# An earlier square root, read-outs moved to VectorE and a check's sums moved into the second pair: a Fourier-mixing and SwiGLU block on one core

## The chip, the cores and the metric

The kernel runs on one core of a Trainium2 chip. The metric is the device time of one execution in microseconds (us). A profile is one further execution, recorded by the hardware profiler. In its rows PE is TensorE (matmuls) and PEld its weight loads, DVE is VectorE, ACT is ScalarE, POOL is GpSimd and SP is SyncE, which here only issues transfers.

## The reference

One row block x of 2048 x 512 goes through two sublayers. All of it is float32.

```python
mod = (_silu(c) @ w_mod).reshape(c.shape[0], 6, 1, -1)
sa, ca, ga, sb, cb, gb = ...               # six vectors of 512
h = _layernorm(x) * (1 + ca) + sa
x = x + ga * (Cr @ h @ Wr - Ci @ h @ Wi)   # real part of a two-dimensional DFT
h = _layernorm(x) * (1 + cb) + sb
x = x + gb * ((silu(h @ w1) * (h @ w3)) @ w2)      # w1, w3: 512 x 1792, w2: 1792 x 512
```

The DFT matrices Cr, Ci (2048 x 2048) and Wr, Wi (512 x 512) are inputs. The kernel uses their mirror symmetry to halve the work, and a check computes whether the inputs have it; if not, a second program, `general`, runs behind the first.

## The kernel before, in words

Each float32 product is made of three matmul passes over a high and a low part: the high part is a rounded copy (ACT, `copy`, L87), the low part is the difference (DVE, `minus`, L90). In the rows `hf`, `h2h`, `th`, `w1h` and so on are such pairs: `h2h`/`h2l` are the two halves of the second layer norm's result, `th`/`tl` are sums of such blocks.

The sequence of 2048 is cut into four blocks t = 0 to 3 of 512 columns; each block is held transposed in two tiles (i = 0, 1) of 128 x 1024. The blocks form two pairs, (0, 2) and (1, 3). "The third block" is t = 2, the second member of the first pair. The hidden width 1792 is cut into seven groups g of 256.

After the DFT, `ln2(t)` computes the second layer norm of a block as a list of small steps: sums over rows and partitions, the square root of the variance (`a6`, ACT, L880, with a table load ahead of it), the reciprocal and its spread (`a6b`, DVE, L883 to L848, tile `stat`), the multiplication of the two tiles by it (`a7`, DVE, `xc`, L96), scale and shift (`a8`, ACT, `xc`, L894), and then the rounding into `h2h` and `h2l` (`chunk_parts`). These steps stand in a queue called `background`. Between the units of PE work the program calls `advance`, which takes steps from that queue as long as a credit in microseconds for DVE and ACT is left; a `pause` ends one call. This decides where a step lands among the other instructions of its engine. Every engine then works strictly in the order in which it was given its instructions. Tiles come from 50 slots that are reused first in, first out, so an instruction that moves also changes which slot a later tile gets.

PE's work around the change is, in this order:

- first products of the first pair, plainly: `up(0,0)`, `up(1,0)` (block 0, groups 0 and 1), eight second products `down` of block 0, then `up(0,2)`, `up(1,2)` (block 2). A second product is six matmuls into one of the PSUM banks 4 to 7, and its result is read out and scaled by `gb` into a tile `y` (ACT, `copy_by`, L335), which POOL's queue adds to DRAM (L1146).
- then twelve `items` (a group g for a pair of blocks). An item has seven products of w1 (a1 to a7) and seven of w3 (b1 to b7) instead of eight each, with sums of weights and of blocks made on DVE. Between them stand eight second products "y" of the item before, now in the two banks 6 and 7 alone. A unit is six matmuls. The order of one item is fixed by a string: `-b7 a1 a2 -b4 -b3 a6 a5 y a7 y y a4 y a3 y b1 y b2 y b6 b5 y`, where a minus marks the item before. a6 adds to the bank of a1, a7 to that of a6 and a4 to that of a7, so each of them starts when ACT or DVE has read what the bank held; b6, b7 and b4 likewise. Items 0 to 4 are the first pair, items 5 to 11 the second.

Of block 1 and block 3 the layer norm runs in the background of items 0 to 2 and 2 to 4.

`judge` (L1003 to L1026) adds up the squares that the check collected: one clearing of a tile by POOL and fifteen small DVE instructions, each of which waits for the one before, ending in the flag `bad`, which is read when everything else is done.

The lines that follow the steps in the profile:

```python
            (0, partition_sums, 1.0, 0.0),
            pause,
            (0, a6, 0.0, 2.8),
            pause,
            (0, a6b, 1.6, 0.0),
```

Of the kernel before, what the change touches and what calls it, by code (L numbers as in the profile page):

```python
# [12 lines left out]
OP = mybir.AluOpType  # L13
# [9 lines left out]
ND = D // P  # L23
# [19 lines left out]
def folded(nc, pools, c, cp, wmr, wmc, x, xt, ctr, cti, wdr, wdi, w1, w3, w2, out):  # L43
# [51 lines left out]
    def times(dst, a, b):  # L95
        nc.vector.tensor_tensor(out=dst, in0=a, in1=b, op=OP.mult)  # L96
# [13 lines left out]
    background = deque()  # L110
# [3 lines left out]
    def step(queue, slots, fn, dve=0.0, act=0.0):  # L114
        queue.append((slots, dve, act, fn))
# [176 lines left out]
    gb = consts.tile([P, ND], F32, name="gb")  # L292
# [41 lines left out]
    def copy_by(dst, src, by):  # L334
        nc.scalar.activation(dst, src, AF.Identity, scale=by)  # L335
# [477 lines left out]
    PAIRS = ((0, 2), (1, 3))  # L813
# [3 lines left out]
    def ln2(t):  # L817
# [69 lines left out]
        def a7(i):  # L887
            rstd = v["s"][:, 1, :].unsqueeze(1).to_broadcast([P, 2, N])
            times(xc[t, i], xc[t, i], rstd)

        def a8(i):
            for q in range(2):
                e = 2 * i + q
                nc.scalar.activation(  # L894
                    xc[t, i][:, q, :],
                    xc[t, i][:, q, :],
                    AF.Identity,
                    bias=sb[:, e : e + 1],
                    scale=cb1[:, e : e + 1],
                )  # L900
# [12 lines left out]


        apart = t != PAIRS[0][0]
        pause = (0, None, 0.0, 0.0)
        for slots, fn, dve, act in (
            (2, a1, 1.2, 0.0),
            (0, a1b, 0.7, 0.0),
            (0, rows, 1.3, 0.0),  # L920
            (1, partition_sums, 1.0, 0.0),
            (1, a2, 1.5, 0.0),
            (1, lambda: a3(0), 1.2, 0.0),
            *[pause] * apart,
            (1, lambda: a3b(0), 0.0, 1.0),
            (1, lambda: a3(1), 1.2, 0.0),
            *[pause] * apart,
            (1, lambda: a3b(1), 0.0, 1.0),
            (0, keep, 0.0, 0.0),
            pause,  # L930
            (0, a4, 1.2, 0.0),
            (0, a1b, 0.7, 0.0),
            (0, rows, 1.3, 0.0),
            (0, partition_sums, 1.0, 0.0),
            pause,
            (0, a6, 0.0, 2.8),
            pause,
            (0, a6b, 1.6, 0.0),
            (0, lambda: a7(0), 1.2, 0.0),
            *[pause] * apart,  # L940
            (0, lambda: a8(0), 0.0, 1.4),
            (0, lambda: a7(1), 1.2, 0.0),
            *[pause] * apart,
            (0, lambda: a8(1), 0.0, 1.4),
            (0, a9, 0.0, 0.0),
        ):
            step(background, slots, fn, dve * (1.4 if apart else 1.0), act)

    def chunk_parts(queue, t, i, more=0):
        def highs():  # L950
            h2h[t, i] = take(F32R, "h2h")
            copy(flat(h2h[t, i]), flat(xc[t, i]))

        def lows():
            h2l[t, i] = take(F32R, "h2l")
            minus(flat(h2l[t, i]), flat(xc[t, i]), flat(h2h[t, i]).bitcast(F32))
            done.add(("h2", t, i))

        step(queue, 1 + more, highs, 0.0, 1.0)
        step(queue, 1, lows, 1.2, 0.0)  # L960

# [150 lines left out]
    ys = {}  # L1112
    down_banks = [4, 4]

    def down_unit(g, pair, t, d, key):
        last = g == NG - 1

        own = pair == 1 and g >= NG - 2
        if not own and d % 2 == 0:
            ys[0] = take(F32, "y")  # L1120

        parts = 2 if own and last and (t, d) == (NT - 1, ND - 1) else 1
        for n in range(parts):
            at = slice(n * N // parts, (n + 1) * N // parts)
            to = bank(down_banks[0] + turn[1] % down_banks[1])[:, at]
            turn[1] += 1
            for q in range(2):
                product(
                    to,
                    [u[:, q, cols(d)] for u in wuse[key]],  # L1130
                    [hf[g, t, q][:, b, at] for b in range(2)],
                    q == 0,
                    q == 1,
                )
            if own:
                xs = xr[t][d // 2][:, d % 2, at]
                nc.vector.scalar_tensor_tensor(
                    xs, to, gb[:, d : d + 1], xs, op0=OP.mult, op1=OP.add
                )
                if last:  # L1140
                    nc.sync.dma_start(out[t, d, :, at], xs)
            else:
                copy_by(ys[0][:, d % 2, :], to, gb[:, d : d + 1])
        if not own and d % 2 == 1:
            y = ys.pop(0)
            nc.gpsimd.dma_start(sums[t, d // 2], y, accum_op=OP.add)  # L1146
            behind(4, lambda: give(y))
            if last:
                behind(8, lambda i=d // 2: store(t, i))
        if d == ND - 1:  # L1150
            for q in range(2):
                give(hf.pop((g, t, q)))
            if t == PAIRS[pair][1]:
                give_w(key)
            if pair == 1 and g == NG - 3:
                load_sums(t)
# [366 lines left out]
    for n, (j, k) in enumerate(steps):  # L1523
        if k == 2:
            load_xt(j + 2)
        if k == 5:
            load_xt(j)
        for m in range(2):
            if todo and todo[0] == (n, m):
                prepare_some(1, n)  # L1530
            if (k, m) == (NK // 2 - 1, 1):
                drain(lambda: ("mod", 0) in done)
            seq_unit(n, m, last_rows if (n, m) == (0, 0) else None)
            load_some(n + 3)
            prepare_some(2 if n == 0 else 1, n + 2)
            square_seq()
            load_some(n + 4)
            if (j, k, m) == (0, NK - 1, 1):
                for t in PAIRS[0]:
                    ln2(t)  # L1540
                    for i in range(2):
                        chunk_parts(background, t, i, 1)
                sum_parts(background, *pair_sums(background, 0))

            if k % (NK // 2) != NK // 2 - 1 or m == 1:
                advance(2.2 if todo else 5.0)
        if n == len(steps) - 3:
            load_w(("w1", 0))
            load_w(("w3", 0))
        if n == len(steps) - 2:  # L1550
            for w in ("w1", "w3"):
                w_high((w, 0))
                w_low((w, 0))
# [40 lines left out]
    for g in range(2):  # L1594
        for d in range(ND):
            down(g, 0, 0, d, ("w2", g))
    judge()
    up(0, 2)
    load_w(("w3", *items[0]))
    weight_jobs(0, "w1")  # L1600
# [8 lines left out]
    turning = len([at for at in items if at[1] == 0])  # L1609
# [11 lines left out]
    def unit(kind, i, n):  # L1621
        g, pair = items[i]
        more = i + 1 < len(items)
# [7 lines left out]
            drain(lambda: ("t", 1, {6: 2, 5: 1, 7: 3, 4: 4}[n]) in done, jobs)  # L1631
        delayed()
        factor(i, "w1" if kind == "a" else "w3", n)
        if (kind, n) == ("a", 1) and more:
            load_w(("w1", *items[i + 1]))
        if (kind, n) == ("a", 6):
# [843 lines left out]
```

## Time and profile before

| | |
|---|---|
| time, three runs | 710.34, 712.18 (median), 712.77 us |
| the profiled execution's own time | 708.46 us |
| its span, first to last instruction | 706.7 us |
| PE busy / weight loads | 686.3 us (97%) / 564.7 us (80%) |
| DVE busy | 548.3 us (78%) |
| ACT busy | 430.8 us (61%) |
| POOL busy | 119.4 us (17%) |
| mean granted TensorE clock | 0.991 |

A row of the timeline gives the start, the duration, the engine, the source line, the operation and the tiles ("out<-in"), and in square brackets how long the engine stood idle before it and what released it. A matmul of 512 columns is recorded with 0.39 us, but they are pipelined: a new one starts every 0.227 us, and the time PE loses is seen in the distance from start to start. The chain of waits follows the end of the program back from instruction to instruction. Stretches of time ("windows") give busy time, number of instructions and granted clock.

### The profile page before, as it was taken

The page shows a single profiled execution, that of the slowest core. Times are in us where ns is not written, and L with a number is a line of the kernel's source. Part 1 is how long each engine was busy: PE and PEld are TensorE (multiplying, and loading weights), DVE is VectorE, ACT ScalarE, POOL GpSimd, SP SyncE. Part 2 cuts the span into 40 slices and gives each one's busy share as a digit, 9 for nine tenths or more (in the row PEclk, how much of TensorE's full clock was granted, in tenths as well). Part 3 has the DMA queues.
Part 4 walks back from the last instruction along what each step waited for, and adds up shares of the span by engine and source line. Part 5 has one row for each costly group of instructions (what it writes and reads, how often), then busy time and mean ns, then how long its engine had stood idle before and what let it go on. Part 6 is the DMA issues. An engine that isn't in the chain of part 4 may idle for free.

```text
span 706.7 us, 8912 instructions
## 1 busy us (share of the span) xinstructions
PE 686.3 (97%) x3152; PEld 564.7 (80%) x3152; DVE 548.3 (78%) x877; ACT 430.8 (61%) x709; POOL 119.4 (17%) x141
## 2 busy tenths in 40 slices
PE   7999999999999999899999999999999999999995
PEld 4898888888888888687888788787788888888784
DVE  5999679997999978579987886896865556664763
ACT  4998865545454655745677676867665565656420
POOL 1320253542524000200100101011010100101000
PEclk9999999999999999999999999999999999999998
DMA  8730299796678521522868558376763847537403
GB/s 266 211 120 1 77 373 328 251 307 229 207 283 287 168 86 41 92 58 64 209 114 199 89 130 153 61 156 137 239 136 73 180 62 175 111 69 162 137 0 124
DMA packets 38100, 108.93 MB, mean 154 GB/s; under 512 B 4896, under 2 KB 5152, under 8 KB 38048
## 3 DMA queue, kind: packets, MB, share of 16 engines
q0 software_dynamic: 12352, 43.00, 29.3%
q1 hardware_dynamic: 25264, 63.98, 27.5%
q10 hardware_dynamic: 432, 1.31, 0.5%
q8 instruction: 26, 0.43, 0.3%
q14 instruction: 26, 0.21, 0.1%
HBM read 76.81 MB, written 33.55 MB: 156 GB/s over the span
## 4 chain that ended last, share of the span: by engine, by line
PE 81%; DVE 7%; ACT 6%; issue 2%; DMA 2%; SPq 1%; ACTq 0%; DVEq 0%
PE bank L100 52%; PE bank L750 25%; PE bank L559 2%; PE bank L598 1%; DMA wmr<-in_wmr 1%; ACT xc L894 1%; PE bank L576 1%; DVE xc L96 1%; SPq L231 1%; ACT hf L87 1%; ACT y L335 1%; DVE v L96 0%; DVE hl L90 0%; ACT hm L501 0%; DMA w<-in_wdi 0%
## 5 line engine op out<-in xcount | busy, mean ns | idle before, releaser
L100 PE MATMUL bank<-hf,w2h 128*128 128x512 f32 (+1 forms) x452 | 140.9, 391 | 0.3
L1146 POOL DMA_DIRECT2D sum<-y x48 | 41.0, 855 | 390.1 <-ACT y L335 373.0
L100 PEld LDWEIGHTS bank<-hf,w2h 128*128 128x128 f32 x452 | 84.3, 188 | 22.1 <-DVE hf L90 3.4
L100 PE MATMUL bank<-hf,w2l 128*128 128x512 f32 (+1 forms) x226 | 87.6, 388 | 0.0
L87 ACT ACTIVATE hf<-v 128x512 fp32r<-128x512 f32 x56 | 35.3, 630 | 67.3 <-DVE v L96 62.7
L335 ACT ACTIVATE y<-bank,gb 128x512 f32<-128x512 f32 x96 | 64.9, 682 | 18.6 <-PE bank L100 18.3
L93 DVE TENSOR_TENSOR v<-bank,x 128x512 f32<-128x512 f32 x36 | 24.7, 685 | 34.9 <-PE bank L100 34.8
L750 PE MATMUL bank<-bh,us 128*128 128x512 f32 x128 | 49.9, 390 | 0.0
L93 DVE TENSOR_TENSOR x<-bank,x 128x512 f32<-128x512 f32 x36 | 24.7, 687 | 32.4 <-PE bank L100 28.7
L750 PE MATMUL bank<-bh,ul 128*128 128x512 f32 x128 | 49.8, 389 | 0.0
L750 PE MATMUL bank<-d,us 128*128 128x512 f32 x128 | 49.8, 389 | 0.0
L750 PE MATMUL bank<-d,uh 128*128 128x512 f32 x128 | 49.8, 389 | 0.0
L750 PE MATMUL bank<-l,us 128*128 128x512 f32 x128 | 49.8, 389 | 0.0
L750 PE MATMUL bank<-l,uh 128*128 128x512 f32 x128 | 49.8, 389 | 0.0
L100 PEld LDWEIGHTS bank<-hf,w2l 128*128 128x128 f32 x226 | 42.4, 188 | 8.4
L90 DVE TENSOR_TENSOR hf<-v,hf 128x512 fp32r<-128x512 f32 x56 | 38.5, 687 | 12.2 <-ACT hf L87 12.1
L170 POOL DMA_INDIRECT re<-in_ctr,mirror x32 | 35.8, 1117 | 66.2 <-DVE ul L90 39.5
L1224 ACT ACTIVATE v<-v 128x512 f32<-128x512 f32 x36 | 22.8, 632 | 38.8 <-DVE v L93 38.8
L87 ACT ACTIVATE x<-bank 128x512 f32<-128x512 f32 x72 | 41.4, 586 | 7.2 <-PE bank L100 6.5
L170 POOL DMA_INDIRECT im<-in_cti,mirror x32 | 32.7, 1023 | 35.3 <-PE bank L750 10.0
L100 PE MATMUL bank<-h2h,w1h 128*128 128x512 f32 x80 | 31.8, 397 | 1.5 <-ACT h2h L87 1.5
L100 PE MATMUL bank<-h2l,w1h 128*128 128x512 f32 x80 | 31.9, 399 | 0.8 <-DVE h2l L90 0.8
(246 smaller groups left out, 1775.2 us busy)
## 6 DMA issues: line engine op xcount, KB each, us to landing
sum<-y POOLq DMA_DIRECT2D x48, 512.0 KB, 5.6
w<-in_w SPq DMA_DIRECT2D x42, 512.0 KB, 4.5
re<-in_ctr SPq DMA_DIRECT2D x32, 256.0 KB, 5.0
im<-in_cti SPq DMA_DIRECT2D x32, 256.0 KB, 5.0
wmc<-in_wmc SPq DMA_DIRECT2D x8, 512.0 KB, 6.3
xr<-in_xt SPq DMA_DIRECT2D x8, 512.0 KB, 7.6
sum<-xr SPq DMA_DIRECT2D x8, 512.0 KB, 6.2
x<-in_x SPq DMA_DIRECT2D x11, 256.0 KB, 4.8
```

Of the source, the lines that this page charges most:

```text
L87: nc.scalar.activation(dst, src, AF.Copy, scale=scale)
L90: nc.vector.tensor_tensor(out=dst, in0=a, in1=b, op=OP.subtract)
L93: nc.vector.tensor_tensor(out=dst, in0=a, in1=b, op=OP.add)
L96: nc.vector.tensor_tensor(out=dst, in0=a, in1=b, op=OP.mult)
L100: nc.tensor.matmul(acc, lhs[a], rhs[b], start=first and n == 0, stop=last and n == len(PASSES) - 1, skip_group_check=more,)
L170: nc.gpsimd.indirect_dma_start(dst, None, rows, bass.IndirectOffsetOnAxis(ap=at, axis=0))
L231: queue.dma_start(raw_w[dt][q * 64 : (q + 1) * 64, m, :], w[i][par::2, q])
L335: nc.scalar.activation(dst, src, AF.Identity, scale=by)
L559: nc.tensor.matmul(halves(hb[k])[:, m, :], sides((hh, hl)[a][k])[:, dt, m, :], wu[dt][:, b, m, :], start=False, stop=dt % 2 == 1 and n == ...
L750: nc.tensor.matmul(acc[what, e], lhs, rhs, start=begin and i == 0, stop=(end or (turn and what == "x")) and i == len(terms) - 1, skip_grou ...
L1146: nc.gpsimd.dma_start(sums[t, d // 2], y, accum_op=OP.add)
L1224: behind(k != 0 or q == 0, lambda: nc.scalar.activation(v, src, AF.Silu))
```

## The change

Only the order of some work and the engine of eight read-outs change; what is computed stays as it was.

1. In `ln2(2)` (`rushed`), the pause ahead of the square root is gone, a pause is put behind `a6b`, and the costs of `a7` and `a8` are set to zero. The rounding of the block comes as `chunk(t, i)`, high part and low part as separate steps between pauses: the first tile is rounded as soon as its scale and shift is done, instead of after both.
2. Of the eight second products of the first pair in groups 0 and 1, numbers 1 to 4 (counted from 0) of each block are read out by DVE (`tensor_scalar`, L1153) in place of ACT. This holds for block 0 (ahead of `up(0,2)`) and for block 2 (in item 0).
3. `judge()` is called behind unit b4 of item 6, which is run at the head of item 7, in place of ahead of `up(0,2)`.

```diff
         apart = t != PAIRS[0][0]
+        rushed = t == PAIRS[0][1]
         pause = (0, None, 0.0, 0.0)
...
             (0, partition_sums, 1.0, 0.0),
-            pause,
+            *[pause] * (not rushed),
             (0, a6, 0.0, 2.8),
             pause,
             (0, a6b, 1.6, 0.0),
-            (0, lambda: a7(0), 1.2, 0.0),
-            *[pause] * apart,
-            (0, lambda: a8(0), 0.0, 1.4),
-            (0, lambda: a7(1), 1.2, 0.0),
-            *[pause] * apart,
-            (0, lambda: a8(1), 0.0, 1.4),
+            *[pause] * rushed,
+            (0, lambda: a7(0), 1.2 * (not rushed), 0.0),
+            *[pause] * (apart and not rushed),
+            (0, lambda: a8(0), 0.0, 1.4 * (not rushed)),
+            (0, lambda: a7(1), 1.2 * (not rushed), 0.0),
+            *([(0, fn, 0.0, 0.0) for fn in (None, chunk(t, 0)[0], None)] if rushed else [pause] * apart),
+            (0, lambda: a8(1), 0.0, 1.4 * (not rushed)),
             (0, a9, 0.0, 0.0),
         ):
             step(background, slots, fn, dve * (1.4 if apart else 1.0), act)
-
-    def chunk_parts(queue, t, i, more=0):
+        if rushed:
+            for fn in (chunk(t, 0)[1], None, chunk(t, 1)[0], None, chunk(t, 1)[1], None):
+                step(background, 0, fn)
+
+    def chunk(t, i):
...
+        return highs, lows
+
+    def chunk_parts(queue, t, i, more=0):
+        highs, lows = chunk(t, i)
...
             else:
-                copy_by(ys[0][:, d % 2, :], to, gb[:, d : d + 1])
+                if pair == 0 and 1 <= g * ND + d <= 4:
+                    nc.vector.tensor_scalar(
+                        ys[0][:, d % 2, :], to, gb[:, d : d + 1], None, op0=OP.mult
+                    )
+                else:
+                    copy_by(ys[0][:, d % 2, :], to, gb[:, d : d + 1])
...
                     ln2(t)
-                    for i in range(2):
+                    for i in range(2 if t == PAIRS[0][0] else 0):
                         chunk_parts(background, t, i, 1)
...
             down(g, 0, 0, d, ("w2", g))
-    judge()
     up(0, 2)
...
         factor(i, "w1" if kind == "a" else "w3", n)
+        if (kind, i, n) == ("b", turning + 1, 4):
+            judge()
```

Three places of the order show what this moves. The first is ACT during the eight second products of block 0, from the table load of the third block's square root on (`s` is that root, `xc` the scale and shift, `y` a read-out). Before:

```order
L880 ACT_TABLE_LOAD
L880 ACTIVATE s_377_2721<-s_377_2721,eps 32x16
L335 ACTIVATE y_2743<-bank_382_2744,gb 128x512
L335 ACTIVATE y_2743<-bank_383_2759,gb 128x512
L335 ACTIVATE y_2769<-bank_385_2770,gb 128x512
L894 ACTIVATE xc_2564<-xc_2564,sb,cb_151 128x512 x2
L335 ACTIVATE y_2769<-bank_386_2780,gb 128x512
L335 ACTIVATE y_2790<-bank_388_2791,gb 128x512
L894 ACTIVATE xc_2611<-xc_2611,sb,cb_151 128x512 x2
L335 ACTIVATE y_2790<-bank_389_2801,gb 128x512
L335 ACTIVATE y_2810<-bank_391_2811,gb 128x512
L87 ACTIVATE h2h_2819<-xc_2564 128x1024
```

ACT at the same place in the changed program:

```order
L880 ACT_TABLE_LOAD
L880 ACTIVATE s_377_2721<-s_377_2721,eps 32x16
L87 ACTIVATE hf_2738<-v_2714 128x512
L335 ACTIVATE y_2750<-bank_382_2751,gb 128x512
L894 ACTIVATE xc_2564<-xc_2564,sb,cb_151 128x512 x2
L87 ACTIVATE h2h_2772<-xc_2564 128x1024
L894 ACTIVATE xc_2611<-xc_2611,sb,cb_151 128x512 x2
L87 ACTIVATE h2h_2796<-xc_2611 128x1024
```

The load and the root now stand ahead of the copy `hf`, which they followed before, and one read-out instead of six stands between the root and the first `h2h`.

The second place is DVE in item 0, around its sums for block 1's layer norm (`xr`, `t`, `r`) and the addition `v` that empties bank 0 of a7 for a4. Before:

```order
L90 TENSOR_TENSOR w3l_3045<-w_406_2925,w3h_3030 128x1024
L90 TENSOR_TENSOR tl_3049<-xc_2259,th_3012 128x1024
L90 TENSOR_TENSOR w3sl_3061<-w3s_3032,w3sh_3047 128x1024
L805 SCALAR_TENSOR_TENSOR xr_2313<-sum_2539,ga,xr_2313 128x512 x2
L805 SCALAR_TENSOR_TENSOR xr_2019<-sum_2539,ga,xr_2019 128x512 x2
L93 TENSOR_TENSOR v_3026<-bank_426_3017,x_3070 128x512
L805 SCALAR_TENSOR_TENSOR xr_2314<-sum_2540,ga,xr_2314 128x512 x2
L805 SCALAR_TENSOR_TENSOR xr_2020<-sum_2540,ga,xr_2020 128x512 x2
L93 TENSOR_TENSOR t_3115<-xr_2313,xr_2314 128x1024
L93 TENSOR_TENSOR t_3115<-t_3115 128x512
```

DVE there in the changed program:

```order
L90 TENSOR_TENSOR w3sl_3045<-w3s_3018,w3sh_3033 128x1024
L805 SCALAR_TENSOR_TENSOR xr_2314<-sum_2540,ga,xr_2314 128x512 x2
L805 SCALAR_TENSOR_TENSOR xr_2020<-sum_2540,ga,xr_2020 128x512 x2
L93 TENSOR_TENSOR v_3012<-bank_427_3003,x_3054 128x512
L93 TENSOR_TENSOR t_3076<-xr_2313,xr_2314 128x1024
L1153 TENSOR_SCALAR y_3058<-bank_444_3079,gb 128x512
L1153 TENSOR_SCALAR y_3088<-bank_446_3089,gb 128x512
L93 TENSOR_TENSOR t_3076<-t_3076 128x512
L826 STREAM_TRANSPOSE t_3076<-t_3076 128x512
L828 TENSOR_REDUCE r_446_3099<-t_3076 128x16
L1153 TENSOR_SCALAR y_3088<-bank_447_3108,gb 128x512
```

One `tl` and half of the `xr` rows have moved ahead of this place, and the read-outs `y` have come in.

The third place is DVE at the head of item 7, behind unit b4 of item 6 (`v<-v,bank` empties its bank; `x<-bank` and the next `v` belong to b3; `hf` is the low part of b4's result). Before:

```order
L96 TENSOR_TENSOR v_4584<-v_4584,bank_738_4731 128x512
L93 TENSOR_TENSOR x_4738<-bank_748_4783,x_4738 128x512
L96 TENSOR_TENSOR v_4583<-v_4583,x_4738 128x512
L93 TENSOR_TENSOR w3s_4853<-w_731_4708 128x256
L90 TENSOR_TENSOR w3s_4853<-w3s_4853,w_731_4708 128x256
L90 TENSOR_TENSOR w3s_4853<-w_731_4708 128x256
L90 TENSOR_TENSOR w3s_4853<-w_731_4708,w3s_4853 128x256
L90 TENSOR_TENSOR hf_4841<-v_4584,hf_4841 128x512
```

In the changed program the same rows stand behind the check's sums, whose last five rows are shown:

```order
L1030 TENSOR_SCALAR own<-sq 1x4
L1032 TENSOR_TENSOR fine<-sq,own 1x4
L96 TENSOR_TENSOR fine<-fine 1x2
L96 TENSOR_TENSOR fine<-fine 1x1
L1035 TENSOR_SCALAR bad<-fine 1x1
L93 TENSOR_TENSOR x_4718<-bank_748_4763,x_4718 128x512
L96 TENSOR_TENSOR v_4563<-v_4563,x_4718 128x512
L93 TENSOR_TENSOR w3s_4853<-w_731_4688 128x256
L90 TENSOR_TENSOR w3s_4853<-w3s_4853,w_731_4688 128x256
L90 TENSOR_TENSOR w3s_4853<-w_731_4688 128x256
L90 TENSOR_TENSOR w3s_4853<-w_731_4688,w3s_4853 128x256
L90 TENSOR_TENSOR hf_4841<-v_4564,hf_4841 128x512
```

All of the check's sums now stand between the `v` of b4 and the low part `hf` of b4's result.

## The prediction

> **What bounds the kernel now.** The first view is the page's line of busy times, the next the waits of PE and of its weight loads.
>
> ```profile
> PE 686.3 (97%) x3152; PEld 564.7 (80%) x3152; DVE 548.3 (78%) x877; ACT 430.8 (61%) x709; POOL 119.4 (17%) x141
> ```
>
> ```profile
> PE bank L100 <- ACT x L87: 1.2, 3, 0.5
> ...
> PEld bank L100 <- DVE hf L90: 3.4, 9, 0.5
> ```
>
> PE is busy for 97% of the span. An edit on DVE or ACT therefore counts only where PE waits for it, or would begin to. The two rows of waits, both short and repeated, say that PE waits where ACT has not yet emptied a bank, and where DVE has not yet made the low part `hf` that a second product needs. The largest single wait is the one the change is about, at the start of `up(0,2)`. The timeline of PE has it:
>
> ```profile
> 294.80 0.39 PE L100 MATMUL bank<-hf,w2l 128*128 128x512 f32 x1
> 296.71 0.51 PE L100 MATMUL bank<-h2h,w1h 128*128 128x512 f32 x1 [1.53 <-ACT h2h L87]
> 297.97 0.79 PE L100 MATMUL bank<-h2l,w1h 128*128 128x512 f32 x1 [0.76 <-DVE h2l L90]
> ...
> 301.03 0.39 PE L100 MATMUL bank<-h2h,w1l 128*128 128x512 f32 x1
> ```
>
> Without a wait the next matmul starts 0.227 us behind the last. From 294.80 to 296.71 PE loses 1.91 − 0.23 = 1.68 us, from 296.71 to 297.97 another 1.26 − 0.23 = 1.03. From 297.97 to 301.03 there are seven starts in 3.06 us where 7 × 0.227 = 1.59 would do: 1.47 lost with no wait shown. The windows tell why (stretch, length, PE busy and its count, those of PEld, DVE, ACT and POOL, granted clock, DMA share, GB/s):
>
> ```profile
> 7.37:10.78 3.41, 2.15 (x11) 1.26 (x10) 1.99 (x7) 2.57 (x6) 0.00 (x0) 1.00 1.04 395
> 10.78:14.19 3.41, 2.32 (x17) 1.95 (x17) 3.30 (x5) 1.85 (x4) 0.00 (x0) 1.00 1.06 257
> ...
> 294.09:297.50 3.41, 1.60 (x6) 0.75 (x4) 0.81 (x1) 3.41 (x6) 0.85 (x1) 1.00 1.00 157
> 297.50:300.91 3.41, 2.94 (x7) 2.36 (x8) 2.73 (x7) 1.96 (x2) 1.03 (x2) 0.50 1.10 177
> ```
>
> The granted clock changes in steps of 3.41 us. A step with 1.81 us of PE idle (53%) was followed by one at 0.50, a step with 1.26 idle (37%) by one at full clock. So a stall here has a second price of 1.47, once it fills about half of such a step. All told this place costs 1.68 + 1.03 + 1.47 = 4.2 us.
>
> **The earlier root and rounding.** The chain of waits that ends in that stall:
>
> ```profile
> 284.41 0.70 DVE v L96
> ...
> 285.78 1.28 ACT L880
> ...
> 287.08 0.32 ACT s L880
> ...
> 290.49 1.10 ACT xc L894 x2
> ...
> 291.92 1.24 ACT y L335 x2
> 293.16 1.41 ACT xc L894 x2
> ...
> 295.61 1.06 ACT h2h L87
> 296.69 1.24 DVE h2l L90
> ```
>
> The sums over which the root is taken are done when DVE turns to `v` at 284.41. The table load nevertheless waits behind `hf` until 285.78. In the changed order load and root stand ahead of `hf`, and the load (1.28) fits in ahead of 284.4, so that the root starts at about 284.4 instead of 287.08, 2.7 sooner. Behind it one read-out `y` stands ahead of the first `h2h` where six stood (order above), as four went to DVE. From the root to the first scale and shift it was 290.49 − 287.08 = 3.4, which gives 287.8; with the one read-out between I take 288.5. Scale and shift (1.10 to 1.5) then end at 290.1, `h2h` (1.06) at 291.2, `h2l` (1.24) at 292.4; the second tile's `h2h`, behind its own scale and shift, at 293.7, its `h2l` at 294.9. PE reaches `up(0,2)` at 294.80 + 0.23 = 295.03 and needs the second tile's low part about 1.6 later. All four pieces are there, and the stall goes whole: **−4.2**. Nothing is late next in this chain; its margin is 2.6 us on the first pair and about 1.7 on the last piece.
>
> **Read-outs on DVE.** DVE reading a bank and scaling it into `y` does not occur in the trace. The nearest groups (line, engine, operation, tiles, count | busy us, mean ns | idle before):
>
> ```profile
> L1137 DVE SCALAR_TENSOR_TENSOR xr<-bank,gb,xr 128x512 f32<-128x512 f32 x15 | 11.2, 749 | 9.0 <-PE bank L100 9.0
> L1137 DVE SCALAR_TENSOR_TENSOR xr<-bank,gb,xr 128x256 f32<-128x256 f32 x2 | 1.0, 484 | 0.6 <-PE bank L100 0.6
> L503 DVE TENSOR_SCALAR hm<-bank,mod 128x256 f32<-128x256 f32 x1 | 0.5, 545 | 0.3 <-ACT hm L501 0.3
> L335 ACT ACTIVATE y<-bank,gb 128x512 f32<-128x512 f32 x96 | 64.9, 682 | 18.6 <-PE bank L100 18.3
> ```
>
> The same operation at half the width takes 0.545, which bounds it below; above, 0.545 + 0.265 = 0.81, if the second half costs what the width costs L1137 (749 less 484). I take 0.75, since L1137 reads the same shape from a bank. ACT is relieved of 8 × 0.68 = 5.5 us, DVE gets 8 × 0.75 = 6.0. In block 0 banks 4 to 7 alternate and the eight units last 1.36 each, so a read-out has some 4 us until its bank is written again: nothing, as long as DVE is not behind by more. In item 0 the banks are two and DVE carries the sums of block 1's layer norm.
>
> ```profile
> 323.50 0.39 PE L100 MATMUL bank<-h2h,w1l 128*128 128x512 f32 x1
> 324.11 0.50 PE L100 MATMUL bank<-th,w1sh 128*128 128x512 f32 x1 [0.23 <-ACT x L87]
> ```
>
> There ACT empties the bank of a1 for a6 behind other work; with less work on ACT this wait, 0.61 − 0.23 = 0.38 and about 0.11 at the restart, goes: **−0.5**. Against it, a read-out on DVE stands behind the `xr` and `t` sums: walking DVE's new order with the durations of before I find y2 ending some 0.1 after PE wants its bank, and with the restart take **+0.2** (0 to 0.5). Near the item's end the row order of ACT and DVE becomes that of item 2 of before, which has no such read-outs:
>
> ```profile
> 407.41 1.07 ACT L87 ACTIVATE x<-bank 128x512 f32<-128x512 f32 x2
> ...
> 408.48 0.39 PE L100 MATMUL bank<-th,w3sh 128*128 128x512 f32 x1
> ```
>
> There ACT's second emptying ends in the moment in which b7 starts, so the margin is at most half of that row, 0.5. In item 0 a read-out of 0.75 more stands ahead on DVE, and the `x` from bank 4 that ACT waits for comes that much later: **+0.5** (0 to 0.75).
>
> **What the order does behind it.** In item 1 the sum `w3sl` now stands ahead of the `v` that empties bank 0, which a4 needs:
>
> ```profile
> 360.66 0.68 DVE L93 TENSOR_TENSOR v<-bank,x 128x512 f32<-128x512 f32 x1
> 361.26 1.21 DVE L90 TENSOR_TENSOR w3sl<-w3s,w3sh 128x1024 fp32r<-128x1024 f32 x1
> ...
> 362.57 0.39 PE L100 MATMUL bank<-th,w1h 128*128 128x512 f32 x1
> ```
>
> Now `v` ends at 361.3, 1.3 ahead of a4; 1.2 later, and with the waits of a6 and a4 gone in item 0 a4 comes 0.4 to 0.5 sooner: 362.6 against 362.15, with the restart **+0.65** (0 to 1.2). Between items 1 and 2 ACT has the table load, the root and the load back to Silu in one row, which in before happens only for block 3; there a4 of PE waits, as it does not for block 1:
>
> ```profile
> 454.77 0.39 PE L100 MATMUL bank<-hf,w2l 128*128 128x512 f32 x1
> 455.43 0.50 PE L100 MATMUL bank<-th,w1h 128*128 128x512 f32 x1 [0.27 <-DVE v L93]
> ```
>
> That is 0.66 − 0.23 = 0.43 and 0.11 at the restart: **+0.55** (0 to 1.1, twice that row).
>
> **The check's sums.** Where they stand before, and what stands at the new place (DVE), and PE there:
>
> ```profile
> 299.70 0.42 DVE L1006 TENSOR_REDUCE sq<-chk 128x8 f32<-128x256 f32 x1 [0.27 <-POOL sq L1005]
> ...
> 302.73 1.20 DVE L90 TENSOR_TENSOR xc<-xc,xc 128x1024 f32<-128x1024 f32 x1
> ...
> 537.61 0.69 DVE L96 TENSOR_TENSOR v<-v,bank 128x512 f32<-128x512 f32 x1 [0.60 <-PE bank L100]
> 538.97 0.69 DVE L93 TENSOR_TENSOR x<-bank,x 128x512 f32<-128x512 f32 x1 [0.67 <-PE bank L100]
> ...
> 541.77 0.68 DVE L90 TENSOR_TENSOR hf<-v,hf 128x512 fp32r<-128x512 f32 x1
> ```
>
> ```profile
> 541.49 0.62 PE L100 MATMUL bank<-hf,w2h 128*128 128x512 f32 x2
> ...
> 542.17 0.84 PE L100 MATMUL bank<-hf,w2h 128*128 128x512 f32 x2
> ```
>
> They hold DVE from 299.70 to 302.73, 3.03 us, though little of it is work: fifteen small instructions, each behind the last. At the old place the stall's aftermath covers them. At the new one DVE is idle from 538.21 (the records overlap a little; the `v` is over 0.60 behind its start) to 538.97, 0.76, so `x` starts at 541.24, 2.27 later, and with it all that follows, the low part `hf` among it: over at 544.7 instead of 542.45. PE's second unit of item 7 wants exactly this `hf`: its pair takes 0.84 where the unit before takes 0.62, so PE waits for it already now and has no margin at all. PE then stands still for **+2.27**. It is 2.6 if DVE has to wait 0.3 for POOL's clearing, as at the old place, and down to nothing if the delay is covered (a rival below). PE's idle time of 2.2 lies on steps of 3.41 that start anywhere: one of them holds 1.26 or more of it at 91% of the positions (2.22 whole in 1.19 of 3.41, and 2 × 0.96 more), 1.66 or more at 68%. The half clock would follow with the price of the third block: **+1.5**. The Trainium skill, in "TensorE: Matmul & The Clock Gate", section "Part 1: The HAM clock gate", has the half rate come after at least one idle window of about 3.4 us; by that rule neither gap would bring it. The trace agrees with the length of the window, 3.41, but not with the rule: one with PE busy for 1.60 of it was enough.
>
> POOL's clearing costs nothing while POOL, 17% busy, has it done ahead. On SP two stores of `xr` move ahead of one weight load, which lands in good time:
>
> ```profile
> w<-in_w SPq DMA_DIRECT2D x42, 512.0 KB, 4.5
> ```
>
> **Sum.** −4.2 − 0.5 + 0.2 + 0.5 + 0.65 + 0.55 + 2.27 + 1.5 = +0.97 on the profiled execution, 708.46, which lies 3.7 below the median of the runs; on the median 712.18 + 0.97 = 713.2. What a measurement of this kernel can tell from no change is about 0.3%, 2.1 us.
>
> **The rivals.** *The check is covered (faster).* If PE does not need the late `hf` where I think, or another order of arrival leaves DVE free earlier, its 2.27 + 1.5 fall away: −2.8, 709.4. For it speaks that DVE has 22% idle; against it the pair of 0.84. From 0.8 us of cover on DVE is late by under 1.5 and the half clock may stay away; from 1.6 on, which leaves 0.67 of the 2.27, it decides: −2.8 + 0.67 = −2.1 is faster.
>
> *The clock holds (no change).* The gap of 2.2 lies across two steps or is too short: 713.2 − 1.5 = 711.7. The Trainium skill's rule above gives this same time for another reason, that no gap below a whole window counts.
>
> *The first pair gets crowded (slower).* From item 0 to item 2 DVE carries the layer norm, 6 us of read-outs are new to the stretch from 286 to 344, and what slips there comes back at each bank: the waits are 0.2 to 0.65 each on my walk, and about 1.3 of idle may fall in one step of 3.41 around a6 and a4 between items 1 and 2, near the 1.26 to 1.81 between which the clock falls. A second half-clocked step (+1.5) and read-outs at 0.81 with the upper ends of the small terms (+0.5) give 715.2. It decides if 1.5 us or more of idle come together there.
>
> **Chances.** The forecast 0.33, the clock that holds 0.14, the covered check 0.25, the crowded first pair 0.28. The forecast and the clock that holds are within 0.3%: same 0.47; faster 0.25, slower 0.28. The likeliest is the forecast, 713.2. By itself it has 711.7 to 714.5, from the ends of the terms. The range has to take in most of the fast and of the slow case: 708.6 to 716.0.
>
> **What would show it.** In the changed profile PE passes from the last second product of block 0 to `up(0,2)` at a distance of 0.23, with the clock at 1.00 there; DVE's read-outs last about 0.75; PE shows a bracket of about 2.2 behind `hf` at the second unit of item 7, with a step at 0.50 behind it; and items 0 to 2 show waits of a few tenths at a4, b7 and y. Wrong would be a stall left at `up(0,2)` (the root not sooner), no bracket in item 7, or a step at 0.50 within the first pair.

## The result, and the profile after

The changed kernel takes as long as the one before: 710.7 us against 711.25 us, medians of 18 runs each; the ratio is 0.9997, 95% interval 0.9986 to 1.0009. A second comparison, on another occasion (12 runs against 34), gave 1.0008 (0.9996 to 1.0020). The kernel before compared with itself gave 1.0007 (0.9996 to 1.0017), so a tenth of a per cent is nothing.

Equal times hide a trade. The profiled execution has a span of 710.3 us; it is a slower one of its kind than that of before (706.7), so single places are compared here, not the spans. First the page's line of busy times, and the waits of PE:

```profile
PE 686.9 (97%) x3152; PEld 563.8 (79%) x3152; DVE 553.3 (78%) x885; ACT 425.9 (60%) x701; POOL 121.6 (17%) x141
```

```profile
PE bank L100 <- DVE hf L90: 2.2, 1, 2.2
PE bank L100 <- ACT x L87: 1.0, 2, 0.5
...
PE bank L100 <- DVE v L93: 0.8, 3, 0.3
```

The waits for `h2h` (1.5) and `h2l` (0.8) are gone, and one for `hf` (2.2) is new. DVE is busy for 5 us more and ACT for 5 us less: these are the eight read-outs. The timeline of PE shows the third block, then item 7:

```profile
296.89 0.39 PE L100 MATMUL bank<-hf,w2l 128*128 128x512 f32 x1
297.12 0.39 PE L100 MATMUL bank<-h2h,w1h 128*128 128x512 f32 x1
297.35 0.39 PE L100 MATMUL bank<-h2l,w1h 128*128 128x512 f32 x1
...
541.56 0.39 PE L100 MATMUL bank<-hf,w2h 128*128 128x512 f32 x1
544.13 0.50 PE L100 MATMUL bank<-hf,w2h 128*128 128x512 f32 x1 [2.19 <-DVE hf L90]
```

PE runs into `up(0,2)` at its own pace of 0.23 us; the stall of before is gone whole. In item 7 the second matmul of a pair stands 2.57 us behind the first. DVE's rows beside it:

```profile
537.00 0.69 DVE L96 TENSOR_TENSOR v<-v,bank 128x512 f32<-128x512 f32 x1 [0.60 <-PE bank L100]
537.61 0.41 DVE L1015 TENSOR_REDUCE sq<-chk 128x8 f32<-128x256 f32 x1
...
540.62 0.67 DVE L93 TENSOR_TENSOR x<-bank,x 128x512 f32<-128x512 f32 x1
...
543.40 0.69 DVE L90 TENSOR_TENSOR hf<-v,hf 128x512 fp32r<-128x512 f32 x1
```

The check's sums hold DVE from 537.61 to 540.62, and `hf` follows 2.8 us behind that as it did before. The windows of PE (stretch, length, PE busy and its count, granted clock, DMA share, GB/s) show the half clock behind it:

```profile
542.19:545.60 3.41, 1.47 (x6) 1.00 0.00 0
545.60:549.01 3.41, 3.41 (x9) 0.50 0.00 0
```

From its first product of block 0 (at 262 us before) to its last matmul PE takes 437.2 us, where it took 436.1, so 1.1 more; in each of these two executions one half-clocked step fell into this part. Added up over the distances from start to start that are above 0.24 us, PE loses 12.0 us there, and 10.95 before; losses "from 262 us on" are counted like this below.

### The profile page after: what moved, and what is told of

Its sections match the earlier page's. It is cut to its first block, busy times and chain, and to the rows that moved or that the text cites. A ratio compares the mean times of both kernels' runs of the same rounds, so it can differ in the third digit from the quotient of the medians.

```text
span 710.3 us, 8925 instructions
## 1 busy us (share of the span) xinstructions
PE 686.9 (97%) x3152; PEld 563.8 (79%) x3152; DVE 553.3 (78%) x885; ACT 425.9 (60%) x701; POOL 121.6 (17%) x141
## 4 chain that ended last, share of the span: by engine, by line
PE 76%; DVE 11%; ACT 7%; issue 2%; DMA 2%; SPq 1%; another core or an unknown queue 1%; ACTq 0%
PE bank L100 49%; PE bank L750 24%; PE bank L559 1%; DMA wmr<-in_wmr 1%; PE bank L598 1%; ACT hf L87 1%; DVE v L96 1%; SPq L231 1%; DVE w3s L90 1%; DVE xc L96 1%; DVE v L93 1%; ACT xc L894 1%; DVE w3sl L90 1%; ACT y L335 1%
## 5 line engine op out<-in xcount | busy, mean ns | idle before, releaser
L335 ACT ACTIVATE y<-bank,gb 128x512 f32<-128x512 f32 x88 | 59.9, 684 | 17.0 <-PE bank L100 16.8
L100 PE MATMUL bank<-h2h,w1l 128*128 128x512 f32 x80 | 31.3, 391 | 0.2 <-DVE w1l L90 0.2
```

What stands on the lines that cost most here:

```text
L100: nc.tensor.matmul(acc, lhs[a], rhs[b], start=first and n == 0, stop=last and n == len(PASSES) - 1, skip_group_check=more,)
```

## The experiments

All times are compared with runs of the kernel before on the same chip. Theory A is the prediction's account (the third block's stall goes, the check's sums cost a wait in item 7 and often a half-clocked step); the other theories differ from run to run, as each expectation says: B is mostly that the wait in item 7 is covered, C that the read-outs carry the gain. "The first run" is the one that follows.

**The check's sums where DVE is idle**

```diff
-        if (kind, i, n) == ("b", turning + 1, 4):
+        if (kind, i, n) == ("a", turning + 1, 7):
             judge()
```

> The changed kernel with the check's sums behind unit a7 of item 6, where VectorE stood idle for 5.5 us, and nothing else altered. Theory A (the account of the prediction: the sums cost 2.3 us of waiting and in most executions a half-clocked step of 1.5 us at their place in item 7): the wait behind hf in item 7 shrinks from 2.2 us to the 0.1 of every other item, no step at 0.50 follows there, and the time is 2.3 to 3.8 us under the changed kernel, about 707 to 708.5 (0.5% under the kernel before). Theory B (the gain at the third block is lost mainly in items 0 to 2, and the wait in item 7 is covered by slack behind it): within 1 us of the changed kernel.

Measured: 707.69 us, ratio 0.9957 (0.9944 to 0.9970). DVE there, and PE in item 7:

```profile
513.46 0.69 DVE L93 TENSOR_TENSOR v<-bank,x 128x512 f32<-128x512 f32 x1
514.06 0.41 DVE L1015 TENSOR_REDUCE sq<-chk 128x8 f32<-128x256 f32 x1
...
519.67 0.69 DVE L93 TENSOR_TENSOR v<-bank,x 128x512 f32<-128x512 f32 x1 [2.53 <-PE bank L100]
```

```profile
540.55 0.84 PE L100 MATMUL bank<-hf,w2h 128*128 128x512 f32 x2
541.23 0.39 PE L100 MATMUL bank<-hf,w2l 128*128 128x512 f32 x1
```

The same sums cost nothing there: DVE still waits 2.53 us for PE behind them, and the pair in item 7 takes 0.84 as in the kernel before. That one move separates this run from the changed kernel, and is worth 0.40% (0.9997 less 0.9957), 2.8 us; the two intervals together leave 1.6 to 4.1. B falls.

**The move of the check's sums alone, in the kernel before**

```diff
-    judge()
     up(0, 2)
...
         factor(i, "w1" if kind == "a" else "w3", n)
+        if (kind, i, n) == ("b", turning + 1, 4):
+            judge()
```

> The kernel before with the check's sums alone moved to their new place (behind unit b4 of item 6). Theory A: PE waits 2.2 us for hf in item 7 as in the changed kernel, and the time is 2.3 us longer than before, 3.8 with a half-clocked step behind it (+0.3% to +0.5%); the third block's stall stays as it was. Theory B (the wait in item 7 is covered): within 1 us of before.

Measured: 713.42 us, ratio 1.0035 (1.0022 to 1.0049), so 2.5 us longer. PE waits 2.2 us for `hf` and has kept its 1.5 and 0.8 at the third block. But in this execution neither gap brought a half-clocked step:

```profile
298.31:301.72 3.41, 1.88 (x8) 1.00 0.92 156
301.72:305.13 3.41, 2.65 (x12) 1.00 1.08 168
544.07:547.48 3.41, 1.84 (x9) 1.00 0.00 0
547.48:550.89 3.41, 2.79 (x12) 1.00 0.00 0
```

The gaps are as long as before, but each lies across two steps, and the fuller one is idle for 1.53 and 1.57 us, less than half. So the step is no fixed price of a gap.

**The check's sums back, all else changed**

```diff
+    judge()
     up(0, 2)
...
-        if (kind, i, n) == ("b", turning + 1, 4):
-            judge()
```

> The changed kernel with the check's sums back ahead of the third block's first products. VectorE has them there in the place where the next four instructions are the sums of the blocks xc, of which the first user is TensorE some 24 us later. Theory A: nothing in that stretch needs VectorE within 3 us, the sums cost PE at most the wait for v of the first products (0.9 us of VectorE's idle time ahead of it, so up to 2 us late, against banks that have slack), and the time is 1.5 to 3.8 us under the changed kernel. Rival C (the sums were moved since they delay the first pair): PE shows a new wait of 1 us or more in the first 10 us of the third block, and the time is within 1 us of the changed kernel.

Measured: 708.73 us, ratio 0.9981 (0.9966 to 0.9996). That is 0.16% under the changed kernel's 0.9997, which the two intervals do not tell apart; in the trace PE loses 2.7 us less than in the changed kernel and 0.9 more than in the first run. No new wait stands in the third block, so C is out. DVE and POOL:

```profile
301.92 0.42 DVE L1015 TENSOR_REDUCE sq<-chk 128x8 f32<-128x256 f32 x1 [2.09 <-POOL sq L1014]
...
304.94 1.20 DVE L90 TENSOR_TENSOR xc<-xc,xc 128x1024 f32<-128x1024 f32 x1
```

```profile
300.85 0.84 POOL L1160 DMA_DIRECT2D sum<-y  x1 [1.97 <-issue]
301.38 0.50 POOL L1014 MEMSET sq<- 128x96 f32 x1
```

With the stall gone, DVE comes to the sums sooner and then waits 2.09 us for POOL's clearing, which stands in POOL's queue behind the transfer of a `y`. What DVE loses shows on PE 20 us later: items 0 to 2 cost 1.0 us more than in the first run, and a wait of 0.23 stands at a6 of item 0. Neither theory had named POOL's queue.

**The earlier root alone**

The kernel before with part 1; the read-outs go to ScalarE as they did, and the check's sums stand where they did.

```diff
-                if pair == 0 and 1 <= g * ND + d <= 4:
+                if False and 1 <= g * ND + d <= 4:
```

> The kernel before with part 1 alone (root sooner, rounding by tiles; all second products read out by ScalarE, check's sums at the old place). Theory A: ScalarE has six read-outs less ahead of the first h2h through the new order, but the read-outs between the steps cost it 0.6 us each, so that the second tile's low part comes about 1 us late: of the 4.2 us of the stall 2 to 3.5 are gained, and nothing is lost in items 0 to 2 from read-outs: 708 to 709.5. Rival C (the root alone brings nothing, the read-outs on VectorE carry the gain): PE waits 2 us or more at the third block, now for the read-outs' banks or for h2h, and the time is within 1 us of before.

Measured: 708.03 us, ratio 0.9965 (0.9953 to 0.9977), as A has it; C falls. Nearly the whole gain is this part's. What is left in front of the third block:

```profile
295.69 0.74 PE L100 MATMUL bank<-hf,w2h 128*128 128x512 f32 x2 [0.34 <-ACT y L335]
```

That is 0.73 from start to start and 0.34 at the restart, 0.6 us lost to a read-out that ScalarE did late; both halves of both tiles are there in time.

**The read-outs alone**

```diff
-                copy_by(ys[0][:, d % 2, :], to, gb[:, d : d + 1])
+                if pair == 0 and 1 <= g * ND + d <= 4:
+                    nc.vector.tensor_scalar(
+                        ys[0][:, d % 2, :], to, gb[:, d : d + 1], None, op0=OP.mult
+                    )
+                else:
+                    copy_by(ys[0][:, d % 2, :], to, gb[:, d : d + 1])
```

> The kernel before with part 2 alone (numbers 1 to 4 of the second products of each block of the first pair read out by VectorE; root, rounding and check's sums as before). Theory A (the prediction's): four read-outs less stand on ScalarE between root and h2h, but the root itself is as late as before, so that h2h comes 0.5 to 1 us sooner and 2 us or more of the third block's stall stay; items 0 and 1 gain 0.5 at a6 and lose 0.2 at y, 0.2 at b7, 0.5 at a4 of item 1 and 0.4 at b7 and b4 of item 1: within 1 us of the kernel before. Theory C (the read-outs carry the gain): 2 us or more under it.

Measured: 712.52 us, ratio 1.0042 (1.0028 to 1.0056): slower than either theory had it. The stall at the third block became longer (PE, then DVE):

```profile
298.24 0.50 PE L100 MATMUL bank<-h2h,w1h 128*128 128x512 f32 x1 [1.94 <-ACT h2h L87]
299.50 0.50 PE L100 MATMUL bank<-h2l,w1h 128*128 128x512 f32 x1 [0.76 <-DVE h2l L90]
```

```profile
290.80 1.21 DVE L96 TENSOR_TENSOR xc<-xc,stat 128x1024 f32<-128x1024 f32 x1
291.93 1.40 DVE L1144 TENSOR_SCALAR y<-bank,gb 128x512 f32<-128x512 f32 x2
293.25 1.22 DVE L96 TENSOR_TENSOR xc<-xc,stat 128x1024 f32<-128x1024 f32 x1
```

With the old root the read-outs stand on DVE between the two tiles' multiplications by `stat`. The second `xc` starts at 293.25, and `h2h`, which in the old order is rounded behind both tiles, comes later for it. But that is the smaller part of the harm. Of the 2.8 us that PE loses more than in the profile of before, 0.7 are at the third block and 2.2 in items 0 to 2. There PE now waits at four places where it did not: at the second product behind a4 (0.61 from start to start), at b7 (0.38) and at b4 (0.43) of item 0, and at a7 of item 1 (0.62). The first and the last of them:

```profile
336.25 0.74 PE L100 MATMUL bank<-hf,w2h 128*128 128x512 f32 x2 [0.33 <-DVE y L1144]
...
362.27 0.51 PE L100 MATMUL bank<-th,w1sh 128*128 128x512 f32 x1 [0.34 <-ACT x L87]
```

The wait of 0.23 at a6 of item 0, which the expectation had go, has stayed. C falls: without the earlier root the read-outs do harm.

**The read-outs for block 0 only, the sums in idle time**

```diff
-                if pair == 0 and 1 <= g * ND + d <= 4:
+                if pair == 0 and t == 0 and 1 <= g * ND + d <= 4:
...
-        if (kind, i, n) == ("b", turning + 1, 4):
+        if (kind, i, n) == ("a", turning + 1, 7):
```

> The changed kernel with the check's sums behind unit a7 of item 6, as in the first run, and with VectorE reading out for block 0 only; in item 0 ScalarE reads out again. If what items 0 and 1 lose belongs to the read-outs in item 0, the waits at y of item 0, b7 of items 0 and 1, b4 and a4 of item 1 go, the 0.5 at a6 of item 0 comes back, and the time is 0.9 us under the first run's 707.7, about 706.8. If it belongs to the earlier layer norm, the waits stay and the time is the first run's or longer.

Measured: 707.26 us, ratio 0.9956 (0.9943 to 0.9970). In the trace PE loses 7.2 us from 262 us on, against 8.3 with the read-outs of item 0 as well. The waits at the second product behind a4 and at b7 of item 0 and at a4 of item 1 are gone, so they belong to the read-outs in item 0. Those at b7 and b4 of item 1 (0.23 and 0.17) have stayed; they stand also in the traces without any read-out on VectorE (the root alone, and the version below with the sums in idle time), so they belong to the earlier root. The a6 wait of item 0 did not return, though ACT reads out there again. In the time the 0.9 us cannot be told from the first run (0.9957); the ratios' intervals are too wide.

**The sums twice, and the sums in two halves**

```diff
         if (kind, i, n) == ("b", turning + 1, 4):
             judge()
+            judge()
```

> The changed kernel with the check's sums done twice at their place in item 7. Theory A (each us that VectorE is held there is a us of PE, and a step of 3.41 us that is idle for half or more brings the half clock): the gap in item 7 grows from 2.2 to 5.2 us, which always fills one step by half or more, so a step at 0.50 follows in every execution: 3.0 us for the gap and 0 to 1.5 more for the clock over the changed kernel, 713.7 to 715.2. If the clock step needs a whole idle window of 3.4 us, the price of the step appears here and not in the changed kernel. Theory B (covered): within 2 us of the changed kernel.

Measured: 715.56 us, ratio 1.0078 (1.0064 to 1.0092). PE's windows:

```profile
543.85:547.26 3.41, 0.00 (x0) 1.00 0.00 0
547.26:550.67 3.41, 2.60 (x6) 0.50 0.00 0
550.67:554.09 3.42, 3.42 (x9) 0.50 0.00 0
```

The pair's second matmul comes 5.58 us behind its first, 3.0 more than in the changed kernel, as A has it. Two steps of half clock follow, where A had counted with one, and the time is 0.4 us over A's upper end. From 262 us on PE loses 16.2 us in this trace, 5.3 more than in the profile of before, which is what the time says (+5.5). Against the changed kernel it is 4.2 more in the traces.

```diff
         if (kind, i, n) == ("b", turning + 1, 4):
-            judge()
+            judge_first()
+        if (kind, i, n) == ("b", turning + 2, 4):
+            judge_second()
```

> The changed kernel with the check's sums cut in two: the first half (up to the four copies, 1.55 us) behind unit b4 of item 6, the second (1.5 us) behind b4 of item 7. Theory A: two gaps of 0.8 to 0.9 us at the second unit y of items 7 and 8 in place of one of 2.2, since the 0.76 of VectorE's idle time covers each half once; no step of 3.41 us is idle for half, so no half clock follows: 1.5 us over the first run's 707.7, about 709.2, and 0.6 (no half clock in the changed kernel) to 2.1 us (always one) under the changed kernel.

Measured: 709.42 us, ratio 0.9992 (0.9983 to 1.0001). PE waits twice for `hf`, and no step at 0.50 follows:

```profile
PE bank L100 <- DVE hf L90: 1.4, 2, 0.8
```

The first 0.76 us of each half are covered, as A has it. Against the sums in idle time the halves cost 0.35% (0.9992 less 0.9957), 2.5 us, where the traces show 1.5 (9.8 us lost from 262 us on, and 8.3); the two intervals leave room for that difference.

**Three checks of the pieces**

The sums moved to the idle place in the kernel before, alone:

> The kernel before with the check's sums moved behind unit a7 of item 6 and nothing else. If the sums cost nothing at their old place (the prediction: the stall's aftermath covers them), the time is that of the kernel before within 0.5 us. If they delay the first products of the third block or item 0, it is 1 us or more under it, and waits at a6 or a4 of item 0 are gone.

Measured: 710.61 us, ratio 1.0011 (0.9998 to 1.0023). Taking the sums away from their old place brings no gain, so they had cost nothing there, as long as the stall was there. The wait at a6 of item 0 is still in the trace.

The earlier root and the sums in idle time, with no read-out on VectorE:

> The kernel before with the earlier root (part 1) and the check's sums behind unit a7 of item 6, without any read-out on VectorE. Against the version that reads out block 0 by VectorE (707.3) it keeps the 0.6 us that PE waited for ScalarE's read-outs in front of the third block. If the read-outs on VectorE are worth only that, it is 0.5 to 1 us longer than that version and 2 us or more under the kernel before; if they are worth nothing, it is the same; if they carry the gain, it is within 1 us of before.

Measured: 706.95 us, ratio 0.9961 (0.9948 to 0.9975). The trace keeps the wait for `y` in front of the third block, and 7.9 us are lost from 262 us on, 0.8 more than with block 0's read-outs; the times don't tell the two apart.

Both kernels once more:

> The changed kernel once more, for its time beside the others on one chip and for a second look at item 7. If the half-clocked step follows the wait in item 7 only where one step of 3.41 us is idle for more than 1.67 us or so, its presence depends on where the steps lie: the wait is 2.2 us again, and the step is there or not by that rule. The time is within 0.3% of the kernel before.

> The kernel before against itself: what the comparison gives for no change (a ratio of 1 within 0.15%), and a second look at the third block. The waits are 1.5 and 0.8 us again, and the half-clocked step behind them is there or not by the idle share of the step of 3.41 us that they fall in.

Measured: ratios 1.0008 and 1.0007, as told above. The windows at the two stalls, the changed kernel in item 7 first, then the kernel before at the third block:

```profile
539.31:542.72 3.41, 1.21 (x6) 1.00 0.00 0
542.72:546.14 3.42, 3.42 (x9) 0.50 0.00 0
```

```profile
298.77:302.18 3.41, 1.80 (x7) 1.00 0.96 148
302.18:305.59 3.41, 2.74 (x11) 1.00 1.06 179
```

In this execution the kernel before has its stall without the half-clocked step. Over the seven starts for which the prediction counted 1.47 us PE loses 0.27 here, so 1.2 of the 1.47 were the clock's, and they are paid only in part of the executions.

## Why the prediction was right, and where its sizes were off

The forecast was no change that can be measured, 713.2 us, and it is none. The way was the one forecast: one stall for another. PE's order is the same in all runs, so its loss can be compared place by place (distance between the same two matmuls, changed kernel less kernel before, in us; the repeated pair is the last two runs):

| place | forecast | first profiles | repeated pair |
|---|---|---|---|
| third block | −4.2 | −4.2 | −3.0 |
| items 0 to 2 | +1.4 | +1.5 | +1.5 |
| second unit y of item 7 and behind | +3.8 | +3.8 | +3.9 |
| all else from 262 us on | 0 | 0.0 | −0.2 |
| together | +1.0 | +1.1 | +2.1 |

The repeated pair differs at the third block, where the kernel before had no half-clocked step that time.

- **The earlier root: −4.2.** Right. The stall is gone (297.12 comes 0.23 behind 296.89), and part 1 alone brings 2.5 us (ratio 0.9965). The chain came as it was walked (ACT, then DVE):

```profile
286.41 0.31 ACT L880 ACTIVATE s<-s,eps 32x16 f32<-32x16 f32 x1 [0.79 <-DVE s L840]
...
290.62 1.52 ACT L894 ACTIVATE xc<-xc,sb,cb 128x512 f32<-128x512 f32 x2 [2.13 <-DVE xc L96]
```

```profile
295.77 1.22 DVE L90 TENSOR_TENSOR h2l<-xc,h2h 128x1024 fp32r<-128x1024 f32 x1
```

Up to here this execution runs 2.1 us behind that of before (block 0's first products start at 264.5 in place of 262.4). Less that, the root starts at 284.3, scale and shift at 288.5, and the last low part ends at 294.9, each within 0.1 us of the forecast. The 288.5 is right by luck: it was got from the time of a read-out on ACT, but ACT has that behind it and waits 2.13 us for DVE's multiplication. Two sizes were off. Of the 1.47 us put down to the half clock 1.2 were the clock's, and they are not paid in every execution. And the read-outs are less needed than the sum of seven against one made them look (the prediction counts six, but the order that stands ahead of it lists seven): without them the root leaves 0.6 us in front of the third block, not a stall.
- **Price of a read-out on DVE: 0.75.** Right. The group in the changed kernel:

```profile
L1153 DVE TENSOR_SCALAR y<-bank,gb 128x512 f32<-128x512 f32 x8 | 5.7, 746 | 0.0
```

- **Items 0 to 2: −0.5, +0.2, +0.5, +0.65, +0.55.** The sum is right and each place is where it was put, but the cause of the first term was not. The second product behind a4 of item 0 loses 0.19 from start to start, b7 of item 0 0.23 (0.5 was counted), a4 of item 1 0.51 and a4 of item 2 0.57:

```profile
360.62 0.50 PE L100 MATMUL bank<-th,w1h 128*128 128x512 f32 x1 [0.24 <-DVE v L93]
...
392.78 0.50 PE L100 MATMUL bank<-th,w1h 128*128 128x512 f32 x1 [0.30 <-DVE v L93]
```

Not foreseen were 0.23 at b7 and 0.17 at b4 of item 1. By the run with read-outs in block 0 alone, the first three of these six belong to the read-outs in item 0 (items 0 to 2 cost 1.1 us less without them); the a4 of item 2 and the two that were not foreseen wait with the root alone too, so they belong to the earlier layer norm.

The wait at a6 of item 0 is gone, as forecast, but not because ACT has fewer read-outs. With the read-outs alone it stays at 0.23, and with no read-out on VectorE at all (earlier root, sums in idle time) it is gone. In the kernel before, ACT rounds a sum of blocks right ahead of the emptying that a6 waits for:

```profile
322.54 1.05 ACT L87 ACTIVATE th<-xc 128x1024 fp32r<-128x1024 f32 x1
323.49 0.57 ACT L87 ACTIVATE x<-bank 128x512 f32<-128x512 f32 x1
```

With the earlier root the last of these roundings is over at 310.6, 11 us ahead of a6. It takes the move of the check's sums as well: with the earlier root and the sums at their old place PE still waits there (0.23, and 0.20 with the root alone), because DVE is late with what ACT rounds first (ACT stands idle for 3.6 us ahead of that rounding, `hf`, and for 2.9 where the wait is gone).
- **The check's sums: +2.27.** Right: the distance within the pair in item 7 grew from 0.34 to 2.57, which is 2.23, and moving the sums away from there gives 0.40% of the time back (0.9997 and 0.9957), 2.8 us. The rival that they are covered is out.
- **The old place and POOL.** Right that the sums cost nothing at their old place while the stall is there. The sentence that POOL has the clearing done ahead holds at the new place; at the old one it fails as soon as the stall is gone, where DVE waits 2.09 us for it.
- **The half clock: +1.5.** The size is right where the step falls (1.6 us), the working was one-sided. The changed kernel had the step in both executions that were profiled; the same gap did not bring it with the move alone. For the kernel before the prediction took it as a fixed part of the 4.2, as its one profile showed it, and gave a chance only to the new gap. Both take that chance. The rival in which the clock holds, 711.7, is therefore one of four pairings of executions and no account of its own: where neither has the step, about 1.2 fall away on one side and 1.6 on the other, and the sum stays within 0.5 us of what it was.
- **The time, and what luck there is in it.** The measured 710.7 lies 1 us under the span that the forecast had by itself, 711.7 to 714.5; only the range that takes in the rivals holds it. Of the 2.5 us between 713.2 and 710.7 the baseline is 0.9: the three runs known at the time had a median of 712.18, the 18 runs 711.25. For the rest, the traces give +1.1 and +2.1, but the two ratios −0.2 and +0.6 us, with intervals of about 0.8 to either side. The granted clock of each run accounts for part of that. Its mean is 0.9921 over 79 runs of the kernel before and 0.9938 over 30 of the changed kernel. A step of 3.41 us at half clock takes 0.0024 off the mean of an execution of 710 us. So the kernel before had some 0.7 steps more on average, which at 1.2 us each is 0.8 us in favour of the changed kernel; this is an estimate, since the mean also counts steps behind the last matmul. The mean is 0.9912 to 0.9922 in the four kernels that keep the third block's stall, and 0.9928 to 0.9951 in those without it, the one with the sums done twice left aside (0.9898). How often the step falls in item 7 stays open: both profiles of the changed kernel have it, but its mean clock is no lower than that of the first run.

The part that carries the trade is thus shown by two moves: the sums alone cost 2.5 us, the rest of the change without them gains 3.0, where the prediction's terms without the sums add up to 2.8. Three versions keep the gain (707.7, 707.3 and 707.0 us, ratios 0.9957, 0.9956 and 0.9961); all three beat both kernels, and they cannot be told from each other.

## What to carry to other kernels

A few microseconds of small instructions are not free on an engine that is idle for a fifth of the time: look in the timeline for a single idle stretch longer than the whole row, as the 5.5 us here, and ask what stands right behind. A wait that already shows a little (0.84 for a pair in place of 0.62) has no margin, and each microsecond put ahead of it is one of the kernel's. When a stall is removed, ask what it had been hiding: here the check's sums, and with them POOL's late clearing. And a term that comes out right need not have the cause it was given: the wait at a6 went away, but the run without read-outs on DVE showed that they had no part in it.

## What was not expected of the hardware

In these traces a half-clocked step of 3.41 us follows a step in which PE was idle for about half, well before it is idle for a whole one, and whether a given gap does it depends on how the steps fall over it. At the stalls of these kernels idle times of 1.81, 1.95, 2.20, 2.51 and 3.41 us in one step were followed by 0.50; 1.53, 1.57 and 1.61 were not. Over all fourteen traces, from the first recorded clock on, no step at full clock with up to 1.61 us of idle was followed by one, and every step with 1.81 or more was. Between them the bound is not sharp: in the kernel before with the sums moved to idle time, 1.63 was followed, and in the repeated changed kernel, at 68 us, 1.80 was not:

```profile
296.81:300.23 3.42, 1.79 (x7) 1.00 1.06 205
300.23:303.64 3.41, 3.41 (x10) 0.50 1.01 159
```

```profile
68.27:71.68 3.41, 1.61 (x8) 1.00 0.00 0
71.68:75.09 3.41, 3.41 (x26) 1.00 0.00 0
```

The Trainium skill, in "TensorE: Matmul & The Clock Gate", section "Part 1: The HAM clock gate", asks for at least one idle window of about 3.4 us. The length of the window agrees with these rows; the condition does not, as 1.81 us of idle were enough.

From a half-clocked step the way back is narrower. With the sums done twice, one with 0.81 us of idle was followed by a second one (the windows of that run above). Of the others ahead of the last matmul, those with 0.55, 0.57 and 0.77 us of idle were followed by a second one, and those with 0.48 or less by full clock.
